# Queries of the first eight pieces: loaded as 32x32 squares and transposed by VectorE, in place of rows transposed by TensorE

**Chip, cores, metric.** One core of a Trainium2 chip; f32 throughout. The metric is the device time of one execution in us. "us" positions in views count from the start of the span.

## The reference

Retention (linear attention with a decay per head) on 8 batches, 8 heads, 576 tokens, head size 64, followed by a two-layer block on 4608 tokens:

```python
scores = q @ k.T / sqrt(64)                       # per batch and head
ret = scores * gamma[h] ** (i - j)   where i >= j, else 0
x = (ret @ v) as (4608, 512)
h = x @ w_in                                      # 512 -> 2048
out = (h * erf(softplus(h))) @ w_out              # 2048 -> 512
```

## The kernel before

The tokens are cut into 36 pieces of 128. A piece needs q and k transposed (head dimension on the partitions) for the scores, and k and v as rows (tokens on the partitions) for the running state. The retention of later pieces is woven into the two-layer block's matmuls; the opening has only the retention of the first pieces and the rounding of the weights to do.

There are two ways to q transposed. **Rows:** the load puts one token on each partition, in runs of 64 values (256 B); TensorE transposes, ScalarE copies out of PSUM. **Squares:** the load puts each block of 32 tokens x 32 dimensions where VectorE's 32x32 transpose finds it; to keep runs long it takes all of four tokens' 64 dimensions less 32 (896 B), so nearly every value is brought twice. The kernel before uses rows for q and k of the first eight pieces (`SQUARES = 8`), squares for the rest:

```python
SQUARES = 2 * PC                                  # PC = 4
SQ = 32
def load_squares(i, name, src):
    t = raw.tile([P, NP, P * D // SQ], FP32, tag=name + "s", ..., bufs=2)
    for b, s0, n, r0 in pieces[i]:
        m = n // SQ * D                           # 256 for a whole piece
        for part in range(P // SQ):               # 4 DMAs of 32 partitions
            e, d0 = part // 2, part % 2 * SQ
            tokens = src[b, e*NP:(e+1)*NP, s0:s0+n, :].rearrange("p (r a) d -> r p (a d)", r=SQ)
            at = r0 // SQ * D
            nc.sync.dma_start(out=t[part*SQ:(part+1)*SQ, :, at:at+m-SQ], in_=tokens[:, :, d0:d0+m-SQ])
    return t

def load_rows(i, name, src, bufs):
    ...                                           # for q: a view of a tile of tag "qs"
    for b, s0, n, r0 in pieces[i]:
        for e in range(2):                        # 2 DMAs of 128 partitions
            heads = src[b, e*NP:(e+1)*NP, s0:s0+n, :]
            nc.sync.dma_start(out=t[r0:r0+n, e::2, :], in_=heads.rearrange("h p d -> p h d"))
    return t
...
def transposes(i):
    ...
    for name in "qk":
        tT = ...
        if i >= SQUARES:
            ...
            nc.vector.transpose(out=tT[:, :, r0:r0+n].rearrange(order, r=SQ), in_=squares[:, :, :, :SQ])
        else:
            pt = ps_at.tile([P, NP, P], FP32, tag="at", name=f"pt_{name}")
            for p in range(NP):
                nc.tensor.transpose(pt[:, p, :], flat(t[name][:, 2*p:2*p+2, :]), ident)
            ...                                   # ScalarE copies pt to tT (q: in another order)
    load(i + 2, "q")
```

All loads are issued by SyncE into one queue. The framework gives these loads eight semaphores in turn, so a load is issued only once the eighth before it has landed.

## Time and profile before

| | before |
|---|---|
| time, median of 3 (range) | 1041.19 us (1038.58 to 1042.32) |
| TensorE busy | 98% of the span |
| VectorE, ScalarE busy | 65%, 37% |
| DMA engines busy, first 40 us | 1.00 |
| start of TensorE's dense stretch | near 85 us |

Read the shares by stage: the 98% of TensorE says where most of the time is spent, but up to 84 us TensorE waits for loads and for VectorE (in the first 17 us it also runs dummy matmuls, meant to keep its clock up). From 85 us it works almost without gaps; I call this the dense stretch, and take as its start the first `PE e` group of eight matmuls on the chain that ended last (84.99 us). The prediction below shows the lines.

### The profile page before, as it was taken

How to read it: one execution, taken by the hardware profiler on the slowest of the kernel's cores; microseconds unless marked ns; L12 is line 12 of the kernel's file. 1: busy time of each engine (PE TensorE's matmuls, PEld its weight loads, DVE VectorE, ACT ScalarE, POOL GpSimd, SP SyncE). 2: the span in 40 equal slices, each digit the busy share in tenths (PEclk: the TensorE clock that was granted, in tenths of full speed). 3: DMA queues.
4: the chain of work that ended last, by engine and by line, in shares of the span. 5: the costliest groups of instructions: out<-in, count | busy, mean ns of one | idle time of the engine just before them, and what ended most of it. 6: DMA issues, size and time to landing. Idle time of an engine off the chain costs nothing.

```text
span 1038.9 us, 15904 instructions
## 1 busy us (share of the span) xinstructions
PE 1018.9 (98%) x6322; PEld 876.6 (84%) x6322; DVE 675.8 (65%) x1063; ACT 388.1 (37%) x477; POOL 125.3 (12%) x122
## 2 busy tenths in 40 slices
PE   9899999899999999999999999999999999999998
PEld 8777877688888888888888888888888888888887
DVE  3998867769777645667665656666666655555555
ACT  2353232231342445443443333434443333333332
POOL 2261222221222100100001000110100000000000
PEclk9999999899999999999999999999999999999999
DMA  9989989979984531543174424353333334444433
GB/s 191 209 212 218 251 179 247 220 184 257 224 195 139 156 147 41 214 172 142 57 255 155 150 114 141 144 206 145 136 122 122 122 121 127 132 132 132 127 88 115
DMA packets 148778, 167.27 MB, mean 161 GB/s; under 512 B 97632, under 2 KB 123360, under 8 KB 140640
## 3 DMA queue, kind: packets, MB, share of 16 engines
q1 hardware_dynamic: 147696, 165.47, 56.4%
q8 instruction: 50, 0.82, 0.4%
q10 hardware_dynamic: 1008, 0.79, 0.3%
q14 instruction: 24, 0.20, 0.1%
HBM read 119.02 MB, written 47.19 MB: 160 GB/s over the span
## 4 chain that ended last, share of the span: by engine, by line
PE 84%; DMA 6%; DVE 4%; SPq 4%; ACT 1%; issue 1%; POOL 0%; DVEq 0%; POOLq 0%; ACTq 0%
PE a L585 22%; PE a L478 22%; PE g L585 11%; PE g L478 11%; PE e L585 6%; PE e L478 5%; PE s L335 2%; PE o L353 2%; SPq L144 2%; DMA raw_qs<-in_q_dram 1%; SPq L130 1%; DMA wraw<-in_moe_w_in_dram 1%; DMA wraw<-in_moe_w_out_dram 1%; DMA raw_ks<-in_k_dram 1%; PE o L376 1%; DMA raw_v<-in_v_dram 1%
## 5 line engine op out<-in xcount | busy, mean ns | idle before, releaser
L478 PE MATMUL a<-x,wa 128*128 128x256 f32 x1120 | 268.0, 383 | 0.0
L478 PEld LDWEIGHTS a<-x,wa 128*128 128x128 f32 x1120 | 212.9, 191 | 29.8 <-issue 0.2
L585 PE MATMUL a<-wb,s 128*128 128x256 f32 x864 | 205.7, 381 | 0.0
L585 PEld LDWEIGHTS a<-wb,s 128*128 128x128 f32 x864 | 163.1, 190 | 23.4 <-ACT o L599 0.7
L99 DVE TENSOR_TENSOR t<-g,t 128x512 f32<-128x512 f32 x70 | 48.4, 691 | 153.2 <-ACT t L508 114.3
L478 PE MATMUL g<-x,wa 128*128 128x256 f32 x560 | 133.2, 381 | 0.5 <-DVE o L99 0.5
L478 PEld LDWEIGHTS g<-x,wa 128*128 128x128 f32 x560 | 105.7, 190 | 15.6 <-DVE o L99 0.9
L99 DVE TENSOR_TENSOR o<-a,o 128x512 f32<-128x512 f32 x108 | 74.3, 688 | 50.4 <-PE a L585 50.4
L503 ACT COPY t<-a 128x512 f32<-128x512 f32 x35 | 20.5, 586 | 188.0 <-PE a L478 188.0
L99 DVE TENSOR_TENSOR t<-t,s 128x1024 f32<-128x1024 f32 x72 | 87.9, 1261 | 0.0
L266 POOL TENSOR_TENSOR wraw<-wraw 128x512 f32<-128x512 f32 x28 | 29.4, 1051 | 463.4 <-DVE wraw L264 252.4
L547 ACT ACTIVATE s<-t 128x1024 f32<-128x1024 f32 x72 | 72.1, 1049 | 28.9 <-DVE t L99 28.9
L99 DVE TENSOR_TENSOR x<-x 128x512 f32<-128x512 f32 x116 | 77.9, 704 | 1.2
L514 ACT COPY t<-a 128x512 f32<-128x512 f32 x35 | 20.5, 586 | 153.0 <-PE a L478 153.0
L551 ACT ACTIVATE s<-s 128x1024 f32<-128x1024 f32 x72 | 72.1, 1049 | 0.4
L585 PE MATMUL a<-wb,t 128*128 128x256 f32 x288 | 68.6, 381 | 1.1 <-DVE t L99 1.1
L585 PE MATMUL e<-wb,t 128*128 128x256 f32 x288 | 68.6, 381 | 0.0
L585 PE MATMUL g<-wb,s 128*128 128x256 f32 x288 | 68.6, 381 | 0.0
L585 PE MATMUL g<-wb,t 128*128 128x256 f32 x288 | 68.3, 380 | 0.0
L478 PE MATMUL e<-x,wa 128*128 128x256 f32 x280 | 66.9, 382 | 0.0
L99 DVE TENSOR_TENSOR o<-g,o 128x512 f32<-128x512 f32 x72 | 49.3, 685 | 24.4 <-ACT o L599 19.6
L99 DVE TENSOR_TENSOR sT<-s,cst 128x512 f32<-128x512 f32 x72 | 46.1, 681 | 26.2 <-PE s L335 26.1
(75 smaller groups left out, 1203.5 us busy)
## 6 DMA issues: line engine op xcount, KB each, us to landing
od<-o SPq DMA_DIRECT2D x54, 512.0 KB, 3.3
x<-xd SPq DMA_DIRECT2D x27, 1024.0 KB, 4.8
o<-od SPq DMA_DIRECT2D x27, 1024.0 KB, 4.9
raw_qs<-in_q_dram SPq DMA_DIRECT2D x96, 112.0 KB, 4.7
raw_ks<-in_k_dram SPq DMA_DIRECT2D x96, 112.0 KB, 4.3
xd<-x SPq DMA_DIRECT2D x9, 1024.0 KB, 5.5
raw_k<-in_k_dram SPq DMA_DIRECT2D x64, 128.0 KB, 4.4
raw_v<-in_v_dram SPq DMA_DIRECT2D x64, 128.0 KB, 4.6
```

Of the source, the lines that this page charges most:

```text
L99: nc.vector.tensor_tensor(out=out, in0=in0, in1=in1, op=op)
L130: nc.sync.dma_start(out=t[part * SQ : (part + 1) * SQ, :, at : at + m - SQ], in_=tokens[:, :, d0 : d0 + m - SQ])
L144: nc.sync.dma_start(out=t[r0 : r0 + n, e::2, :], in_=heads.rearrange("h p d -> p h d"))
L266: engine.tensor_tensor(out=r_f, in0=high_f, in1=r_f, op=ALU.mult)
L335: nc.tensor.matmul(ps[e][:, p, :], lhsT=t["kT"][heads[e], p, :], rhs=t["qT"][heads[e], p, :], start=True, stop=True)
L353: nc.tensor.matmul(o[p % 2][heads[(e + p) % 2], p // 2, :], lhsT=t["v"][:, 2 * p + e, :], rhs=t["sT"][:, e, p, :], start=(p < 2), stop=(no ...
L478: nc.tensor.matmul(acc[:, j * TH : (j + 1) * TH], lhsT=weights["wa", self.g][:, a, d, j * P : (j + 1) * P], rhs=x[self.g, self.c][a][:, d, :],
L503: nc.scalar.copy(out=self.t1[:, 1], in_=self.a)
L514: nc.scalar.copy(out=self.t2[:, 0], in_=self.a)
L547: nc.scalar.activation(self.s[:, j], t, AF.Softplus)
L551: nc.scalar.activation(self.s[:, j], self.s[:, j], AF.Erf)
L585: nc.tensor.matmul(acc[:, tp, :], lhsT=left[:, j * TH + tp * P : j * TH + (tp + 1) * P], rhs=weights["wb", self.g][:, b, j, :], start=(sta ...
```

## The change

Its intent: take q's transposes and copies off TensorE and ScalarE in the opening, use half as many packets for q, and drop a special case. k of these pieces stays as it was.

```diff
-    def load_rows(i, name, src, bufs):
-        if name == "q":
-            t = raw.tile([P, NP, P * D // SQ], FP32, tag="qs", name="raw_q", bufs=bufs)
-            t = t.rearrange(...)                  # cut
-        else:
-            t = raw.tile([P, H, D], FP32, tag=name, name=f"raw_{name}", bufs=bufs)
+    def load_rows(i, name, src):
+        t = raw.tile([P, H, D], FP32, tag=name, name=f"raw_{name}")
...
-                if name == "q" and i < SQUARES:
-                    t["q"] = load_rows(i, "q", q, 2)
-                elif name == "q":
+                if name == "q":
                     t["qs"] = load_squares(i, "q", q)
-                    t["ks"] = load_squares(i, "k", k)
+                    if i >= SQUARES:
+                        t["ks"] = load_squares(i, "k", k)
...
-            if i >= SQUARES:
+            if name + "s" in t:
                 ...                               # VectorE transposes squares
             else:
-                ...                               # q: ScalarE's copy in another order
                 nc.scalar.copy(out=tT, in_=pt)
```

More of the change, by code (lines that the diff above doesn't have):

```diff
@@ L133, in load_squares @@
         return t
-    def load_rows(i, name, src, bufs):
-        if name == "q":
-            t = raw.tile([P, NP, P * D // SQ], FP32, tag="qs", name="raw_q", bufs=bufs)
-            t = t.rearrange("p a x -> p (a x)")[:, : H * D].rearrange("p (h d) -> p h d", h=H)
-        else:
-            t = raw.tile([P, H, D], FP32, tag=name, name=f"raw_{name}", bufs=bufs)
+    def load_rows(i, name, src):
+        t = raw.tile([P, H, D], FP32, tag=name, name=f"raw_{name}")
         for b, s0, n, r0 in pieces[i]:
@@ L151, in load @@
                 src = {"q": q, "k": k, "v": v}[name]
-                if name == "q" and i < SQUARES:
-                    t["q"] = load_rows(i, "q", q, 2)
-                elif name == "q":
+                if name == "q":
                     t["qs"] = load_squares(i, "q", q)
-                    t["ks"] = load_squares(i, "k", k)
+                    if i >= SQUARES:
+                        t["ks"] = load_squares(i, "k", k)
                 elif name == "v" or len(pieces[i]) == 1:
-                    t[name] = load_rows(i, name, src, 4)
+                    t[name] = load_rows(i, name, src)
     load(0)
@@ L317, in transposes @@
             else:
-                pt = ps_at.tile([P, NP, P], FP32, tag="at", name=f"pt_{name}")
+                pt = ps_at.tile([P, NP, P], FP32, tag="at", name="pt")
                 for p in range(NP):
                     nc.tensor.transpose(pt[:, p, :], flat(t[name][:, 2 * p : 2 * p + 2, :]), ident)
-                if name == "q":
-                    nc.scalar.copy(
-                        out=tT.rearrange("p h (a r) -> p h a r", r=SQ), in_=pt.rearrange("p h (r a) -> p h a r", r=SQ)
-                    )
-                else:
-                    nc.scalar.copy(out=tT, in_=pt)
+                nc.scalar.copy(out=tT, in_=pt)
         load(i + 2, "q")
```

## The prediction

> **What bounds the kernel now.** I read the page's slices first, then the busy times by stage, then the chain that ended last cut to the first 140 us, and last the groups of instructions and the DMA view in narrow windows.
>
> The slices show a kernel bound by TensorE for nearly all of its span, with the DMA engines full in the first third only:
>
> ```profile
> PE   9899999899999999999999999999999999999998
> DVE  3998867769777645667665656666666655555555
> DMA  9989989979984531543174424353333334444433
> ```
>
> The stages, whose columns are the busy time of PE, PEld, DVE, ACT and POOL (instructions in brackets), granted clock, DMA share and GB/s:
>
> ```profile
> 0.00:40.00 40.00, 35.41 (x434) 30.22 (x434) 20.43 (x42) 11.89 (x19) 9.66 (x15) 1.00 1.00 187
> 40.00:84.00 44.00, 39.13 (x360) 31.36 (x358) 42.05 (x67) 19.02 (x28) 18.36 (x16) 1.00 0.95 233
> 84.00:130.00 46.00, 46.00 (x454) 37.60 (x452) 38.91 (x66) 13.58 (x18) 7.68 (x9) 1.00 1.04 225
> 130.00:200.00 70.00, 64.09 (x600) 51.65 (x599) 46.92 (x83) 21.11 (x26) 16.79 (x18) 0.95 0.96 208
> ```
>
> Up to 40 us the DMA share is 1.00 while VectorE is half idle. From 40 to 84 us VectorE is busy for 42.05 of 44 us. From 84 us TensorE has no gap for 46 us, and after 200 us it idles 4.65 of 838.9 us. So the end is set by when the dense TensorE work starts, near 84 us, plus what stalls it between 130 and 200 us. The chain of the opening (start, us, what) says the same:
>
> ```profile
> 16.36 3.84 DMA raw_v<-in_v_dram
> ...
> 22.43 6.33 DMA raw_v<-in_v_dram
> ...
> 31.96 6.18 DMA wraw<-in_moe_w_in_dram
> ...
> 38.22 0.69 ACT wa L246
> ...
> 38.94 0.44 DVE wa L251
> ...
> 84.99 1.92 PE e L585 x8
> ```
>
> Loads end the waits until 38 us: rows of q, k, v and, behind them in the same queue, the first input weights. Then the weights' rounding runs on ScalarE and VectorE, and from 85 us TensorE follows on itself. All eight pieces that the change touches are loaded before 45 us, so it acts only on this opening.
>
> **What the Trainium skill says.** Three places bear on it.
> - "DMA: Bandwidth & Descriptors", Specifications, puts the least transfer for line rate at 512 B and says that smaller ones cost a read-modify-write. By this the new 896 B runs should beat the old 256 B runs. The trace disagrees: a window with only row loads (8 to 14 us, 256 B packets) and one that is 88% square loads by packets (152 to 155 us) move the same bytes per second. I go by the trace.
>
> ```profile
> DMA packets 5322, 1.34 MB, mean 223 GB/s; under 512 B 5321, under 2 KB 5321, under 8 KB 5321
> DMA packets 871, 0.69 MB, mean 230 GB/s; under 512 B 105, under 2 KB 871, under 8 KB 871
> ```
>
> - "VectorE: DVE Perf Modes", The three transpose paths: VectorE transposes 32x32 blocks only, into SBUF, and TensorE a whole 128x128 into PSUM. The trace agrees in form: the squares are laid out by the loads, and TensorE's result needs a copy out of PSUM by ScalarE. Its 311 and 390 ns are for bf16; the f32 durations below are used.
> - "Perfetto Trace Analysis", What "DMA-bound" means, distinguishes full DMA engines from a full issuing sequencer. Here the engines are full (share 1.00), but the sequencer is not far off: two row issues take 0.98 us and four square issues 1.80 to 1.87 us in the order of time.
>
> **The change part by part.** Rows from the groups, and the issue table:
>
> ```profile
> L320 PE MATMUL pt_q<-ident,raw_q 128*128 128x128 f32 x32 | 5.4, 296 | 2.1 <-DMA raw_q<-in_q_dram 2.0
> L322 ACT COPY qT<-pt_q 128x512 f32<-128x512 f32 x8 | 4.7, 586 | 21.4 <-PE pt_q L320 21.4
> L314 DVE STREAM_TRANSPOSE qT<-raw_qs 128x512 f32<-128x512 f32 (+1 forms) x32 | 19.9, 631 | 10.6 <-DMA raw_qs<-in_q_dram 10.6
> raw_qs<-in_q_dram SPq DMA_DIRECT2D x96, 112.0 KB, 4.7
> raw_q<-in_q_dram SPq DMA_DIRECT2D x16, 128.0 KB, 4.6
> ```
>
> 1. Removed: 32 TensorE transposes, 5.4 us busy, and 8 ScalarE copies of 586 ns, 4.7 us. TensorE waits for loads and VectorE in the opening (in places on purpose: it is fed dummy matmuls there), and ScalarE is busy under half of it. On the path: 0.
> 2. Added: 8 VectorE transposes. The mean of 631 ns mixes whole and half tiles; a whole 128x512 takes 700 ns. That is 5.6 us. Six fall before 39 us, where VectorE is half idle and waits for loads: 0. In VectorE's order of the changed program the seventh stands after the last rounding of the input weights and the eighth between the first two roundings of the output weights, thus inside the full stretch: 2 x 0.70 = 1.4 us on the path.
> 3. Changed: the loads of q. A piece was 2 DMAs of 128 KB (1024 packets of 256 B), and becomes 4 of 112 KB (512 packets of 896 B), because each square load brings columns that it doesn't need: 448 KB for 256 KB. At the rates above, 262,144 B / 223 GB/s = 1.18 us and 458,752 B / 230 GB/s = 1.99 us: +0.8 us of a full queue per piece. The issue time grows by the same +0.85 us, at the same time, so it isn't added.
> 4. How it reaches the path: six pieces' q stand in the queue ahead of the last two input-weight loads, which start the full VectorE stretch: 6 x 0.8 = 4.9 us. All eight stand ahead of the first output-weight loads: 8 x 0.8 = 6.5 us.
> 5. Sum: by VectorE 4.9 + 1.4 = 6.3 us; by the queue alone 6.5 us. The two run beside each other, so the start of the dense stretch moves by about 6.4 us, not by the sum. I take off 0.9 us, as VectorE has 2 us of gaps between 40 and 84 us and the queue falls to a third of its load near 60 us, where it can catch up. That leaves +5.5 us, or 0.5%.
>
> After 84 us nothing changes: later pieces are loaded and transposed by the same instructions as before. A delay of TensorE's dense work that arises before 84 us goes to the end nearly undiminished.
>
> **The rivals.**
> - The loads cost nothing (same time, 1039 to 1042 us). For it: half as many packets, and the skill's 512 B line; the queue's share near 16 us drops to about 0.7, so there is some room. Against it: the measured bytes per second are the same, and the bytes grow.
> - Relief: TensorE and ScalarE lose 10 us of work, a PSUM buffer out of every six of this pool's uses before 45 us falls away, and each piece's scores start sooner (2 to 4 us faster). Against it: TensorE then only waits for k, which is loaded after q.
> - The opening worsens more than its sum: 8 square and row DMAs per piece instead of 6, each issue held until the eighth DMA before it has landed, so a longer landing time stalls the queue; or VectorE, which runs in order, holds finished outputs behind a transpose whose q hasn't landed. Up to twice the sum: +10 to +13 us. Against it: row DMAs already run so, and the TensorE stood behind the same load before.
> - A gap of TensorE long enough to drop its clock. The skill ("TensorE: Matmul & The Clock Gate", Part 1) has it halve after some 3.4 us of idleness. The trace agrees that it happens: the granted clock is 0.95 from 130 to 200 us. That loss of 3.4 us (5% of 70) may vanish or come twice.
>
> **Range and chances.** 1041.2 + 5.5 = 1046.7 us. The runs before spread over 3.7 us, the load estimate may be off by half (3 us), and the clock by 3.4 us: 1041.5 to 1052.5. For 2% the change would have to move 20.8 us, three times the sum, or more than all the work it removes. So faster 0.01, within 2% 0.96, slower 0.03.
>
> **What would show it.** Right: the last two input-weight loads land some 5 us later than 39 and 40 us; the first dense TensorE stretch starts near 90 instead of 84 us; busy times after 200 us are unchanged; DMA bytes rise by 8 x 0.19 = 1.5 MB and packets fall by 8 x 512 = 4096; VectorE's busy time rises by 5.6 us, TensorE's falls by about 5. Wrong: if the input weights land at the same time, the rates of the loads were misjudged; if they land late but the dense stretch starts on time, there was slack in VectorE's stretch; if it starts late and the end doesn't move, a later stall took it up (130 to 200 us); if the end moves by over 12 us, look for a new wait on q's squares in VectorE, or a second clock drop.

## The result

| | before | after |
|---|---|---|
| time, median of 4 (range) | 1039.88 us (1038.45 to 1042.32) | 1045.35 us (1045.24 to 1047.82) |
| ratio | | 1.0056, 95% interval 1.0029 to 1.0083 |

A ratio is the mean time of one kernel's runs over that of the other's in the same rounds, so not quite the ratio of the medians. The change costs 0.56%, some 5.8 us: clear of noise, though within the 2% that count as the same time.

The page of the kernel after, three rows of the slices:

```profile
PE   8698999999999999999999999999999999999998
DVE  3799868868777645666666656666667555555555
DMA  9989989999994532444174433453333333444424
```

TensorE's first four slices fell from 9, 8, 9 and 9 to 8, 6, 9 and 8; past the opening the rows look as before. The stages of the kernel after (same columns as in the prediction):

```profile
0.00:40.00 40.00, 29.80 (x319) 25.69 (x320) 17.67 (x34) 6.67 (x10) 7.75 (x14) 0.87 1.01 187
40.00:84.00 44.00, 39.01 (x398) 31.44 (x399) 42.46 (x73) 18.84 (x27) 16.98 (x15) 1.00 0.95 214
84.00:130.00 46.00, 43.66 (x408) 35.16 (x408) 40.22 (x62) 12.41 (x16) 9.33 (x10) 1.00 1.03 229
130.00:200.00 70.00, 66.56 (x641) 54.07 (x642) 50.42 (x88) 23.42 (x30) 15.04 (x16) 1.00 0.97 219
```

Up to 40 us VectorE executed 34 instructions where it had executed 42, although transposes of q had been added to its work: everything is later. The DMA share and rate are the same, 1.00 and 1.01 at 187 GB/s. The DMA view of the first 40 us, before and then after, says what the full queue carried:

```profile
DMA packets 21480, 7.49 MB, mean 187 GB/s; under 512 B 20325, under 2 KB 20325, under 8 KB 21477
```

```profile
DMA packets 16905, 7.47 MB, mean 187 GB/s; under 512 B 13111, under 2 KB 16183, under 8 KB 16903
```

A fifth fewer packets, and the same bytes. (The second profiles of the two kernels have 187 and 194 GB/s, so the other packets bring at most 4% more.) And the change asks for 6 x 0.197 = 1.18 MB more ahead of the last input weights. The order of time on ScalarE shows when the last input weights were there, as the first step of their rounding waits for them. Before:

```profile
40.47 0.69 ACT L246 ACTIVATE wa<-wraw 128x512 f32<-128x512 f32 x1 [0.98 <-DMA wraw<-in_moe_w_in_dram]
```

After, 6.04 us later:

```profile
46.51 0.69 ACT L241 ACTIVATE wa<-wraw 128x512 f32<-128x512 f32 x1 [1.05 <-DMA wraw<-in_moe_w_in_dram]
```

And the chain of the kernel after has q's squares and what waits behind them where before had v and the weights; the piece that was at 84.99 us before is at 93.29:

```profile
15.23 6.46 DMA raw_qs<-in_q_dram
...
22.76 5.01 DMA wraw<-in_moe_w_in_dram
...
31.63 5.42 DMA raw_qs<-in_q_dram
...
38.88 5.00 DMA wraw<-in_moe_w_in_dram
...
93.29 1.92 PE e L575 x8
```

One profile is one execution. Both kernels were profiled twice; the second profile of before is 1034.8 us long, the second of after 1039.1 us, against 1038.9 and 1045.8. So I give means of two where a step is judged by a microsecond or two:

| milestone, mean of two profiles | before | after | shift | predicted |
|---|---|---|---|---|
| last input-weight load landed | 40.7 us | 45.5 us | +4.8 | +4.9 |
| second output-weight load landed | 51.7 us | 58.1 us | +6.5 | +6.5 |
| TensorE starts its dense stretch | 85.3 us | 92.7 us | +7.4 | +5.5 |
| end | 1036.9 us | 1042.4 us | +5.6 | +5.5 |

The totals moved as counted: bytes read from HBM 119.02 to 120.60 MB (+1.58), VectorE 675.8 to 681.7 us (+5.9). Packets fell by 3840: the predicted 4096, less 256 four-byte packets that the trace has more of, 16 for each of the 16 more DMAs. TensorE's busy time fell by 1.0 us in the first pair of profiles and by 3.8 us in the second, against about 5 predicted; at half clock the same work takes longer (eight 128x256 matmuls 3.71 us where others take 1.92), and the first profile of after has 10 us of that in its opening.

The second profile of after happens to be of its fastest run (1040.86 us; the other nine took 1044.4 us or more), so the end is better judged by the ratio, +5.8 us.

### The profile page after: what moved, and what is told of

It is laid out like the page before. It is cut to its first block, busy times and chain, and to the rows that moved or that the text cites.

```text
span 1045.8 us, 15862 instructions
## 1 busy us (share of the span) xinstructions
PE 1017.9 (97%) x6290; PEld 874.9 (84%) x6290; DVE 681.7 (65%) x1071; ACT 383.7 (37%) x469; POOL 125.4 (12%) x122
## 3 DMA queue, kind: packets, MB, share of 16 engines
HBM read 120.60 MB, written 47.19 MB: 160 GB/s over the span
## 4 chain that ended last, share of the span: by engine, by line
PE 78%; DMA 12%; DVE 5%; SPq 3%; issue 1%; ACT 1%; POOL 0%; DVEq 0%; POOLq 0%; ACTq 0%
PE a L575 21%; PE a L468 21%; PE g L575 11%; PE g L468 10%; PE e L575 6%; PE e L468 5%; DMA raw_qs<-in_q_dram 4%; DMA raw_ks<-in_k_dram 2%; SPq L130 2%; PE s L325 2%; DMA raw_v<-in_v_dram 1%; PE o L343 1%; DMA cst<-in_decays_dram 1%; DMA xd<-x 1%; DMA wraw<-in_moe_w_in_dram 1%; DMA raw_k<-in_k_dram 1%
## 5 line engine op out<-in xcount | busy, mean ns | idle before, releaser
L575 PEld LDWEIGHTS g<-wb,s 128*128 128x128 f32 x288 | 55.4, 194 | 10.1 <-DVE t L99 2.2
```

The costliest lines, as they stand in the source:

```text
L575: nc.tensor.matmul(acc[:, tp, :], lhsT=left[:, j * TH + tp * P : j * TH + (tp + 1) * P], rhs=weights["wb", self.g][:, b, j, :], start=(sta ...
```

## The experiments

Theory: **the queue.** The extra bytes of the squares delay the weights. Rivals: **VectorE** (its added transposes), **the number of DMAs** (4 for 2 per q), and **TensorE's clock** (it idles more in the opening). All times are medians; effects in us are ratio less one, times 1038.9. The two halves and the counts are told from each other by kernels that compute something wrong; they move data of the same shape.

**The load half alone (wrong result).**

```diff
-                    t["q"] = load_rows(i, "q", q, 2)
+                    t["q"] = load_squares(i, "q", q)
...
-   nc.tensor.transpose(pt[:, p, :], flat(t[name][:, 2*p:2*p+2, :]), ident)
+   nc.tensor.transpose(pt[:, p, :], t[name][:, p, :P] if name == "q" else flat(...), ident)
```

> The load half of the change alone: q of the first eight pieces comes as squares (4 x 112 KB for 2 x 128 KB), but TensorE and ScalarE still transpose and copy it, as before; the result is wrong on purpose. Queue theory (the 1.5 MB more in a full queue is the cost): +4.5 to +6 us against before, input weights' last load landing near 45 instead of 40 us. VectorE theory (the added transposes are the cost): 0 to +1 us. Clock theory (TensorE lost 32 transposes, fell idle in the opening and its clock dropped; that is the cost): 0 to +2 us, as TensorE keeps its transposes here.

Measured: 1046.41 us, ratio 1.0068 (1.0049 to 1.0087): +7.1 us, a little over what was expected. The last input weights landed at 46.5 us. The loads alone cost at least all of the change; VectorE's and the clock's theory each allowed at most 2 us here. For VectorE this settles it. For the clock it doesn't: TensorE keeps its transposes in this run, but its clock fell all the same (0.91 granted up to 40 us, 0.96 from 84 to 130 us).

**The VectorE half alone (wrong result).**

```diff
+            if name == "q" and i < SQUARES:       # rows, transposed as if they were squares
+                nc.vector.transpose(
+                    out=tT.rearrange("p h (a r) -> p h a r", r=SQ),
+                    in_=t["q"].rearrange("p (h e) (x r) -> p h (e x) r", e=2, r=SQ))
-            if i >= SQUARES:
+            elif i >= SQUARES:
```

> The VectorE half alone: q of the first eight pieces comes as rows as before, and VectorE transposes those rows in 32x32 blocks in place of TensorE and ScalarE; the result is wrong on purpose. Queue theory: 0 to +1.4 us (two of eight transposes of 0.70 us lie in VectorE's full stretch). VectorE theory: +4 to +6 us. Clock theory: +4 to +6 us, as TensorE loses the same 32 transposes as in the change.

Measured: 1037.45 us, ratio 0.9994 (0.9971 to 1.0016): -0.6 us, no effect that five rounds can tell. The relief of TensorE and ScalarE and the load on VectorE are all in this kernel; together they are worth between -3.0 and +1.7 us. Its chain holds a surprise, though. The start of the dense stretch in the second profile of before and in this one:

```profile
85.62 1.92 PE e L585 x8
```

```profile
88.10 1.92 PE e L590 x8
```

It comes 2.5 us later, and the end doesn't. The stage from 130 to 200 us shows where this is made up, for the second profile of before and for this kernel:

```profile
130.00:200.00 70.00, 66.86 (x636) 54.20 (x635) 51.80 (x88) 22.85 (x29) 20.17 (x20) 1.00 1.01 215
```

```profile
130.00:200.00 70.00, 69.41 (x684) 56.29 (x680) 54.45 (x93) 22.97 (x29) 21.72 (x20) 1.00 0.98 215
```

Before, TensorE is without work for 3.1 us of this stage, mostly waiting for VectorE's k, whose squares come late; here for 0.6 us. So there is a second place where TensorE meets the queue. A late start that leaves the queue alone is taken off the wait there.

**As many DMAs as the change, with the bytes of before.** Two ways: before's rows in four DMAs (correct), and the change's four square DMAs cut short (wrong).

```diff
-                heads = src[b, e * NP : (e + 1) * NP, s0 : s0 + n, :]
-                nc.sync.dma_start(out=t[r0 : r0 + n, e::2, :], in_=heads.rearrange("h p d -> p h d"))
+                for m in range(0, NP, 2) if name == "q" else [None]:
+                    ...                           # for q: heads m, m+1 of this half in a DMA of their own
```

> The kernel before with q's rows of the first eight pieces in four DMAs of 64 KB (two heads each) instead of two of 128 KB: as many DMAs per piece as the change has, with the bytes and packets of before; correct result. If the number of DMAs or their issue (0.43 to 0.5 us each, +1 us a piece) is what costs: +4 to +6 us. If the bytes in the queue are (queue theory): 0 to +1.5 us.

```diff
+                w = P if name == "q" and i < SQUARES else m - SQ
-                    out=t[...][:, :, at : at + m - SQ], in_=tokens[:, :, d0 : d0 + m - SQ]
+                    out=t[...][:, :, at : at + w], in_=tokens[:, :, d0 : d0 + w]
...
+                    if i < SQUARES:
+                        squares = t["qs"][:, :, :P].rearrange("p h (a d) -> p h a d", d=SQ)
```

> The changed kernel with its four square DMAs per piece cut to 128 of 224 columns (64 KB each): the change's number of DMAs and packets, but before's bytes; the data are wrong on purpose. Bytes as the cost: 0 to +2 us. Number of DMAs as the cost: +4 to +6 us. The split rows gave +3.2 us with this count and these bytes, so if both count, about +3 us.

Measured: 1042.21 us, ratio 1.0031 (1.0014 to 1.0047), +3.2 us, for the split rows; 1040.63 us, ratio 1.0020 (1.0003 to 1.0037), +2.1 us, for the short squares. Both are between what the two theories expected: the number of DMAs costs something where the bytes are few. The DMA view of the first 40 us, for the split rows and then the short squares, shows that the engines were not full:

```profile
q1 hardware_dynamic: 20738, 7.19, 84.4%
```

```profile
q1 hardware_dynamic: 17776, 7.31, 85.4%
```

The third number is the queue's share of the 16 engines. It is 99.4% before and 100.2% after the change. What keeps them short, the split rows' order of time on SyncE suggests:

```profile
9.72 1.97 SPq L148 DMA_DIRECT2D raw_q<-in_q_dram  x4
11.73 1.02 SPq L148 DMA_DIRECT2D raw_k<-in_k_dram  x2
12.79 1.06 SPq L148 DMA_DIRECT2D raw_v<-in_v_dram  x2
```

The next piece follows at 13.95 us. SyncE issues without a pause, and gets 768 KB out in 4.23 us, 186 GB/s, less than the 223 GB/s that the queue took of such rows when it was full. So here the issuing itself was the limit. The rule of eight may be one later: seven others were in flight at 3 of the 31 issues from 6 to 24 us, and at 8 of the 21 from 24 to 40 us. No run holds the two apart.

**The change's bytes in as few DMAs as before (wrong result).**

```diff
+            if name == "q" and i < SQUARES:
+                for e in range(2):                # 64 partitions x 4 heads x 224 values, tokens overlap
+                    ...
+                    nc.sync.dma_start(out=t[e * 2 * SQ : (e + 1) * 2 * SQ, :, : m - SQ], in_=wide)
+                continue
```

> The changed kernel with each piece's squares in two DMAs of 64 partitions (224 KB each) in place of four of 32 (112 KB each): the change's bytes and packets, but as few DMAs as before; the data are wrong on purpose. Bytes in the queue as the cost: +4 to +6 us against before, as the change. Number of DMAs as the cost (a new issue waits until the eighth before it has landed): 0 to +2 us.

Measured: 1045.23 us, ratio 1.0064 (1.0052 to 1.0076): +6.6 us. With two DMAs for four the whole cost is still there. So in the change it is the bytes. The number of DMAs counts only while the engines aren't full, and the bytes of the squares keep them full.

**Half of it: pieces 0 to 3 alone.**

```diff
-                if name == "q" and i < SQUARES:
+                if name == "q" and 4 <= i < SQUARES:
```

> The change for pieces 0 to 3 alone, 4 to 7 as before; correct result. Queue theory: half the bytes, 4 x 0.8 = +3.3 us on the last input-weight loads, and none of its transposes in VectorE's full stretch: +2 to +3.3 us. VectorE theory (only those in the full stretch cost): 0 us. If the cost comes from the first two pieces' start alone: about the whole +5.5 us.

Measured: 1040.72 us, ratio 1.0022 (1.0004 to 1.0039): +2.3 us, correct. Four pieces cost about half, as bytes would; none of their transposes lies in VectorE's full stretch.

**TensorE's clock.** The changed kernel with more dummy matmuls, and the changed kernel again beside it.

```diff
         elif what == "k":
-            keep_busy(2)
+            keep_busy(5)
```

> The changed kernel with five dummy TensorE matmuls instead of two at each of the places in the opening that keep it busy. In the profile of the change TensorE ran at half clock for 3.4 us from 13 us and for 6.8 us from 30 us, which before didn't. Clock theory (this drop is part of the cost): 2 us or more faster than the change, so +0 to +3.5 us against before. Queue theory (TensorE waits for loads there anyway): within 1 us of the change, +5 to +7 us against before.

> The changed kernel once more, in five rounds, as the reference for the run with more dummy matmuls on the same chip: +5 to +7 us against before.

Measured: 1047.01 us, ratio 1.0070 (1.0055 to 1.0085), with more dummies, against 1044.86 us, ratio 1.0051 (1.0033 to 1.0068), for the change as it is. More dummies don't help. They didn't keep the clock up either: its profile still shows half clock for 6.8 us from 12.7 us and 3.4 us from 46.8 us. So this run doesn't hold the clock fixed; what speaks against the clock as the cause is the VectorE half above, whose opening also shows two half-clock stretches of 3.4 us (from 12.0 and from 39.3 us) and which costs nothing; the second profile of the change has two such stretches in its opening as well, and no more. A small part of the cost may still be the clock's.

**The other direction.** If bytes ahead in the queue cost, then more pieces as rows should gain: each saves k's squares (448 KB that are loaded beside k's rows) and the surplus of q's.

```diff
-    SQUARES = 2 * PC
+    SQUARES = 10                                  # and 12, 16
...
-                elif name == "v" or len(pieces[i]) == 1:
+                elif name == "v" or len(pieces[i]) == 1 or i < SQUARES:
...                                                # ScalarE's copy of q by segments, for split pieces
```

> The change's direction reversed: from the kernel before, pieces 8 and 9 too are loaded as rows (q and k) and transposed by TensorE, 10 pieces instead of 8; correct result. Queue theory: their k squares (448 KB each) aren't loaded at all and q shrinks, 2 x 2.8 us of queue, and VectorE loses 2 x 1.8 us in its full stretch: -2 to -4 us. If TensorE is what limits between 60 and 84 us (it gains 2 x 1.2 us there): 0 to +2.5 us.

> As the run with ten pieces as rows, but twelve; correct result. Pieces 10 and 11 are transposed near or after 84 us, where TensorE has no gaps, so their 2 x 1.2 us of TensorE add to the end, against 2 x 2.8 us of queue. Queue theory: -2 to -5 us; TensorE-bound theory: +2 to +5 us.

> As the runs with ten and twelve pieces as rows (-6.6 and -6.3 us), but sixteen: pieces 12 to 15 are transposed after 100 us, where TensorE has no gaps. If TensorE's added transposes count one for one there (1.2 us a piece, 4 pieces) while the queue no longer holds it up: about +5 us against twelve, so -1 to -2 us against before. If the queue or VectorE still hold TensorE up: -6 us or better.

Measured, all correct:

| pieces as rows | median | ratio (interval) | effect |
|---|---|---|---|
| 8 (before) | 1038.7 and 1038.8 us | 1 | |
| 10 | 1032.67 us | 0.9937 (0.9924 to 0.9950) | -6.5 us |
| 12 | 1032.37 us | 0.9939 (0.9926 to 0.9952) | -6.3 us |
| 16 | 1035.80 us | 0.9966 (0.9953 to 0.9978) | -3.5 us |

Ten gained more than expected, and beats both kernels. Twelve also gained more than the queue's theory said (-2 to -5 us), and nothing like what a bound TensorE would have made of it. For sixteen the outcome lies between the two expectations. The gain of ten doesn't come from an earlier start of the dense stretch, which is at 85.3 us as before. Its stages from 84 us:

```profile
84.00:130.00 46.00, 46.00 (x459) 37.61 (x456) 39.13 (x66) 13.57 (x18) 7.12 (x8) 1.00 1.02 224
130.00:200.00 70.00, 70.00 (x676) 57.00 (x675) 55.91 (x94) 23.53 (x30) 21.65 (x21) 1.00 0.95 219
```

TensorE has no gap from 84 to 200 us, where before had 3.1 and 5.9 us of gaps in its two profiles. It is the same second place as in the VectorE half: the queue's lead there grew (table below). These runs move bytes and VectorE's work together, so they don't by themselves say which of the two gained. At sixteen, TensorE has no gaps from 84 to 200 us either, so that its added transposes there can only lengthen it; that this is the whole difference to ten is not shown.

**Before, profiled again.**

> The kernel before once more, for a second profile of it. In its first profile TensorE stopped for 4.16 us near 185 us and then ran at half clock for 6.8 us; in the two profiles of the change the start of the dense stretch came 8.3 and 7.1 us late, but the end 6.9 and 0.2 us. If that stop belongs to before in every execution: it is here again, the time is 1038 to 1041 us, and the change's late start is made up there. If it comes and goes: it is smaller or missing here, with a time of 1036 to 1039 us, and the part made up is chance between executions.

Measured: one execution, 1036.60 us. TensorE's longest stop past the start of the dense stretch, in the first and in this profile, from the order of time:

```profile
189.31 2.08 PE L335 MATMUL s<-qT,kT 64*128 64x128 f32 x16 [4.16 <-DVE kT L314]
```

```profile
187.13 1.16 PE L335 MATMUL s<-qT,kT 64*128 64x128 f32 x16 [1.72 <-DVE kT L314]
```

The bracket is the idle time before the instruction. The stop is there in both, of different length; in the first profile TensorE then ran 6.8 us at half clock from 188 us, which this one hasn't. The two executions of one kernel end some 4 us apart, near the size of the effect studied. Only means over rounds can be compared to a microsecond, and a single profile not.

**The second meeting, over all profiles.** The chain of before, just ahead of the first of these two lines, shows what TensorE waits for there: k's squares, which stand in the queue behind a load of output weights (the sixth).

```profile
175.06 6.90 DMA wraw<-in_moe_w_out_dram
...
181.97 5.99 DMA raw_ks<-in_k_dram
...
188.08 1.09 DVE kT L314
```

How late that load of output weights lands tells how late the queue is at this place. Shifts in us against the means of before's two profiles (85.3, 181.8 and 1036.9 us):

| profile | start of the dense stretch | sixth output-weight load landed | end |
|---|---|---|---|
| VectorE half | +2.8 | -1.3 | -2.0 |
| short squares | +5.3 | +0.8 | +2.6 |
| pieces 0 to 3 alone | +4.1 | +1.8 | +1.8 |
| split rows | +3.9 | +3.6 | +3.5 |
| the change, first and second profile | +8.0, +6.8 | +7.5, +2.9 | +8.9, +2.2 |
| loads alone | +6.9 | +8.1 | +8.2 |
| squares in two DMAs | +8.1 | +7.9 | +7.6 |
| the change with more dummies | +9.4 | +9.0 | +8.6 |
| 10, 12, 16 pieces as rows | 0.0, -0.4, -0.7 | -4.3, -5.1, -7.7 | -5.4, -3.4, -3.3 |

The end goes with the queue to within 2 us (but for sixteen as rows), and not with the start of the dense stretch. The queue can make up lost time as well: in the second profile of the change the eighth piece's v landed 6.1 us late, near 54 us, and the load at 185 us only 2.9. This is a comparison of profiles and not an experiment: loads also wait for buffers that VectorE and TensorE free, so the queue doesn't run on its own.

## Why the prediction was right

The time (1045.35 us for 1046.7) and the direction were right, and so was the cause. Some terms of the sum were wrong, in opposite directions; that the total came out so close is partly luck. By its own steps:

- **What bounds the opening.** Right: the queue's share was full and stayed full, and the weights came later by what was put ahead of them.
- **Removed work, worth 0 on the path.** Right: the VectorE half, which has the whole relief, measured -0.6 us with an interval on both sides of 0 (-3.0 to +1.7 us).
- **The bytes, +0.8 us a piece.** Right, and best supported: the landings moved by 4.8 and 6.5 us where 4.9 and 6.5 were predicted, and of the two-by-two set (bytes and number of DMAs) the two with many bytes cost 5 to 7 us with either count. The rate by bytes was taken from a window with only rows and one with mostly squares; had the 512 B line been trusted in its place, the forecast would have been the first rival, no cost. The agreement to a tenth is luck: the two profiles of the change put the last input weights 3.9 and 5.8 us late, and over the five profiles with its loads (the two, loads alone, two DMAs, more dummies) the mean is 46.0 us, 5.6 us later than the 40.4 us of the six with rows as before (before twice, the VectorE half, and 10, 12 and 16 pieces as rows).
- **VectorE's 2 x 0.70 us.** Too small for the start of the dense stretch: alone it moved by 2.5 us. Three transposes lie in the full stretch, not two (the sixth runs just ahead of the third rounding), and 3 x 0.70 = 2.1 us is most of it. And wrong for the end, where it is worth nothing.
- **Slack, -0.9 us.** Wrong: the dense stretch started 7.4 us late, not 5.5. VectorE's gaps took nothing up: from 40 to 84 us it was busy 42.05 and 41.97 us before, 42.46 and 41.81 after.
- **"A delay of TensorE's dense work that arises before 84 us goes to the end nearly undiminished."** This step failed. Of 7.4 us 5.6 arrive, and of the VectorE half's 2.5 us none. By the table above, a delay passes the second meeting with the queue about so far as the queue itself is late there, and that was 7.5 and 2.9 us in the two profiles of the change, 5.2 on average. This error makes the end earlier than the step would have it, the two before it later, so the sum came out better than its terms.
- **Rivals.** "The loads cost nothing" and "relief" fell with the two halves. The number of DMAs is real (+3.2 us for the split rows; the short squares' +2.1 us holds VectorE's half as well) but only when it leaves the engines unfilled, which the change doesn't. The clock's drops are there in most profiles, at changing places; no run held the clock fixed.

Open: why TensorE's stop near 187 us varies between executions, and how much of the gain with ten pieces as rows is the queue's and how much VectorE's.

## What to carry to other kernels

Where a load queue is full, price a new layout by its bytes at the rate that your trace shows for such packets, and ask what stands behind it in the queue. Work taken off an engine that waits for those loads was worth nothing here. And before carrying a delay to the end, look for the next place where the two streams meet: in these profiles the end went by how late the queue was there, and not by how late its consumer had started.

## What the Trainium skill lacked or had wrong

- "DMA: Bandwidth & Descriptors", Specifications: 512 B as the least transfer for line rate. Here 256 B rows moved at 223 GB/s and 896 B squares at 230 GB/s, and the two openings, with 21480 and 16905 packets, both at 187 GB/s (187 and 194 in the second profiles). Packets above the line earned 0 to 4%.
- The same page gives a cost of issuing a load for all shapes alike, and no time by shape. From SyncE, uncontended, it took 0.43 us for 128 packets of 896 B and 0.51 us for 512 packets of 256 B.
- "VectorE: DVE Perf Modes", The three transpose paths: no figure for f32, nor for the order of the output. A 128x512 f32 transpose took 703 ns (q) and 1097 ns where the result is written in a scattered order (k).
- No page that I read gives the size of load below which one issuing engine falls behind full DMA engines: with q in four DMAs of 64 KB SyncE got a piece out at 186 GB/s, issuing without a pause, and the queue's share in the first 40 us was 84.4%; with two of 128 KB it was 99.4%.
